# Attention scores from the fourth chunk on as float16 pairs over 64 rows, in a newly written order

## The chip, the cores and the metric

The kernel runs on one core of one Trainium2 chip. The metric is the device time of one execution in microseconds (us). The core has a matrix engine (TensorE, in the profile PE, its weight loads PEld), a vector engine (VectorE, DVE), a scalar engine (ScalarE, ACT), GpSimd (POOL) and a queue engine (SyncE, SP) which issues all transfers here.

## What is computed

The input is `q`, `k`, `v` of 4 batches, 8 heads, 768 positions, 64 channels. Each position attends to 96 local and 8 global positions; a two-layer network follows.

```
scores = q @ k.T / sqrt(64) + bias; scores = where(keep, scores, -1e9)
a = exp(scores - max); a = a / sum(a); attn = a @ v
x = attn as 3072 rows of 512
h = x @ w_in            # 512 x 2048
g = h * tanh(log(1 + exp(h)))
out = g @ w_out         # 2048 x 512
```

## The kernel before

The 3072 positions are 12 chunks of 256 (`ci`), three to a batch. A chunk has two halves of four heads, which are loaded apart (`G = 2*ci + g`: 24 loads of `q` and `k`), and eight score tiles `t`, so 96 in all: tile `t` belongs to chunk `t // 8`, and is for one pair of heads and one block of 128 queries. The pair's two heads lie on the two halves of the 128 partitions. For each head, `scores` multiplies 64 rows of `q` (128 columns, loaded as weights) with 64 rows of `k` (256 columns; 128 in the first block of a batch). One tile so takes two matmuls, one on each half of the rows, into two PSUM tiles `sc0` and `sc1`. Both are float32; each such matmul shows as two weight loads and two matmuls in the trace.

The other products take float16 pairs: a number is split into a high and a low float16 part, and high x high, high x low and low x high are added up in PSUM. Such is `weigh` (attention times `v`), `moe_in` (`ph`: 24 matmuls of 256 columns for a block `m`; 96 blocks, 8 to a chunk) and `moe_out` (`po`: 12 matmuls of 512 columns a block). The weights come as 64-bit numbers in 32 pieces of 512 KB and are turned to float16 pairs by `exponent_w`, `sign_w`, `join_w`, `high_w`, `low_w`, through four buffers each named `wc` and `ws`. Once the last piece is through, these buffers are idle.

No scheduler moves anything: every engine runs in the order of a written string, `PROGRAM`. A word is a letter and an index, a prime sends the step to DVE instead of ACT or POOL. The letters that matter here: `q` `v` `w` loads, `s` scores, `t` bias and row maximum (DVE), `y` exponential (ACT), `g` `p` high and low part of it, `X` its transposing transfer, `W` weigh, `A` to `E` the five steps of a weight piece, `i` moe_in, `o` moe_out, `z` `Z` high and low part of the activation, `L` `M` masks, `N` (new) their rescaling, `a` `b` (new) high and low part of `q`, `c` `d` (new) of `k`. The indices of `a` to `d` count from one more than `G`.

The first two chunks' blocks stand side by side: i0, i8, i1, i9 and so on to i7, i15; i16 and what follows is in rising order. By i16 all weight pieces are converted.

Of the kernel before, what the change touches and what calls it, by code (L numbers as in the profile page):

```python
# [114 lines left out]
def windowed(st, tc, loc):  # L115
# [88 lines left out]

    def split_v(ci):
        if ci < NC:
            for f in (high_v, low_v, window_v):
                f(ci)
# [36 lines left out]


# [256 lines left out]
    def flags():  # L503
# [25 lines left out]
        y15 W11 p13' g14 C4 X13 p14' D4 B5 A5 X14 t16 E4 i0 g15 q5 C5 y16 p15 D5 E5 W12 h2 X15 s17 j0 W13 l2 w6 W14 g16 R2 p16 x2 t17 T2 m0 s18 y17
        U2 X16 t18 u0 W15 R3 n0 s19 V2 y18 g17' T3' w7 r0 t19 p17 A6 w8 s20 U3 g18 X17 y19 G0 W16 t20 p18 V3 g19 H0 s21 y20 p19 X18 t21 z0 A7' s22  # L530
        y21 X19 B6 B7 w9 t22 Z0 W17 A8' g20 o0 C6 y22 w10 C7 D6' g21 D7' E6' w11 p21' i8 g22' B8 E7' A9 w12 B9 i1 C8 j8 C9 D8 w13 m8 A10 B10 u8 p20
        D9 s23 n8 p22' W18 w14 j1 W19 X20 t23 E9 r8 A11' y23 X21 m1 A12' G8 u1 X22 C10 n1 H8 E8 D10 r1 w15 i9 E10' A13 G1 z8 B11 A14 w16 g23 H1 Z8
        W20 j9 W21 p23' z1 i2 m9 X23 R4 Z1 u9 n9 B12 q6 T4 B13 W22 r9 U4 j2 G9 V4 m2 H9 u2 w17 W23 C11 z9 i10 B14 n2 Z9' A15 w18 C14 r2 D11 C13 D14
        s24 G2 j10 w19 R5 E11 D13 m10 o8 T5 E13' u10 H2 E14 w20 n10 t24 B15 r10 y24 o1 C12 w21 G10 z2 C15 A16 Z2' D12 A17 w22 H10 o9 A18 E12' D15
        z10' B16 g24 w23 B17 i3 B18 E15' w24 Z10' B19 i11 C18 j3 A19' w25 D18 m3 C16 u3 E18' D16 A20' n3 o2 p24' w26 C19 j11 X24 r3 U5 D19 m11 G3 V5
        u11 E19' o10 n11 H3 E16 r11 v3 C17 z3 B20 A21 i4 G11 A22 q7 A23 C20 D17 H11 Z3 D20 E17' z11 i12 q8 j4 E20' A24 B21 Z11' h3 C21 o3 m4 q9 D21
        A25' l3 u4 j12 E21' n4 x3 o11 m12 r4 B22 u12 B23 v4 n12 C22 r12 C23 s25 D22 G4 D23 E22' A26 H4 E23 t25 i5 z4 G12 y25 B24 g25 H12 Z4 w27 z12
        i13 C24 j5 Z12' D24 m5 B25 u5 B26 n5 w28 o4 C25 j13 w29 r5 C26 D25 B27 A27 G5 o12 w30 C27 D26' D27' m13 H5 E26 u13 z5 s26 E24' n13 A28' i6
        t26 Z5 r13 A29 G13 y26 B28 H13 E25 A30 w31 o5 j6 C28 g26 z13 m6 B29 D28 u6 Z13' i14 B30 n6 C29 r6 C30 D29' o13 D30' j14 G6 m14 H6 E30 u14 z6
        E28' s27 n14 Z6' i7 r14 q10 t27 p26 G14 y27 E27' g27' s28 j7 B31 o6 m7 p27' u7 H14 E29 n7 z14' r7 i15 A31' Z14' C31 G7 D31 h4' o14 H7 j15  # L540
        p25 l4 X25 z7 m15 X26 t28 E31 u15 i16 y28 Z7' X27 n15 r15 x4 g28' o7 p28 j16 G15 m16 H15 u16 v5 z15' n16 i17 Z15 Q0 r16 Y0 G16 s29 j17 H16
        o15 t29 z16' y29 m17 Z16' u17 g29 i18 n17 p29 Q1 r17 Y1 W24 G17 W25 j18 s30 X28 m18 W26 H17 u18 W27 X29 o16 t30 z17 n18 Z17 y30 r18 i19 g30
        G18 p30' H18 X30 z18' s31 j19 Z18 i20 t31 q11 m19 y31 u19 s32 g31 n19 W28 p31' W29 W30 j20 t32 o17 X31 r19 R6 y32 m20 T6 g32' G19 u20 s33 U6
        n20 o18 t33 V6 r20 H19 y33 G20 z19 p32' i21 Z19' X32 H20 g33' z20 p33' i22 Z20' j21 X33 m21 u21 n21 W31 r21 s34 R7 j22 o19 h5 t34 l5 y34 m22
        s35 x5 g34 T7' G21 u22 W32 o20 t35 p34 n22 H21 r22 q12 y35 U7 G22 z21 i23 g35' H22 p35 V7 z22 Z21' X34 Z22' s36 j23 o21 X35 m23 t36 u23 v6
        n23 y36 s37 r23 i24 t37 g36 p36 y37 G23 X36 g37 s38 H23 j24 p37 o22 t38 z23 Z23 y38 m24 g38' u24 i25 p38 n24 r24 G24 s39 H24 j25 o23 m25 q13
        z24 t39 u25 Z24 y39 n25 s40 g39' Q2 p39 i26 t40 r25 Y2 y40 G25 H25 s41 j26 z25' o24 m26 t41 Z25 u26 n26 y41 s42 r26 i27 t42 G26 y42 H26 z26
        i28 j27 Z26 m27 u27 s43 j28 W33 n27 m28 q14 W34 u28 W35 W36 r27 o25 n28 G27 X37 r28 H27 G28 X38 z27' i29 H28 Z27 X39 z28' Z28' i30 j29 g40
        m29 u29 p40 g41 n29 g42' W37 X40 t43 p41 W38 j30 o26 r29 R8 p42 y43 X41 G29 T8 X42 m30 U8 o27 u30 H29 V8 g43 n30 z29' p43 r30 Z29' s44 G30
        W39 W40 t44 X43 W41 i31 R9 y44 H30 g44' z30 T9' h6' s45 j31 Z30' W42 W43 l6 o28 t45 p44 x6 m31 y45 U9 X44 s46 u31 o29 g45 t46 V9 n31 p45'  # L550
        y46 v7 X45 r31 s47 g46 G31 o30 q15 t47 p46 H31 y47 z31' X46 Z31' i32 g47' p47' X47 s48 j32 i33 t48 m32 y48 u32 g48' p48' n32 s49 j33 o31 t49
        r32 m33 y49 G32 u33 H32 g49 W44 n33 p49 W45 X48 Q3 i34 R10 z32 X49 T10' r33 Z32 Y3 W46 G33 j34 W47 U10 o32 h7 m34 V10 H33 u34 l7 z33 n34 i35
        R11 Z33 x7 r34 G34 T11 H34 U11 v8 o33 z34 j35 V11 Z34 m35 u35 o34 n35 r35 G35 H35 i36 z35 Z35' i37 j36 m36 u36 n36 s50 r36 o35 j37 G36 m37
        H36 u37 t50 n37 z36' i38 r37 Z36' y50 G37 H37 g50' o36 z37' j38 p50 m38 X50 Z37' u38 i39 n38 r38 G38 H38 o37 j39 z38 m39 u39 Z38' n39 s51
        r39 i40 G39 q16 t51 H39 y51 i41 z39 g51' j40 p51 m40 X51 Z39 u40 o38 j41 n40 m41 u41 r40 n41 G40 W48 W49 W50 r41 H40 W51 s52 G41 i42 z40'
        t52 Z40 H41 y52 z41' g52' Z41' i43 j42 p52 m42 X52 u42 n42 o39 j43 r42 m43 u43 G42 n43 H42 s53 Q4 W52 z42' i44 t53 Z42 r43 Y4 y53 G43 H43
        g53 s54 p53 j44 o40 X53 m44 t54 u44 n44 y54 s55 z43 g54' o41 t55 q17 r44 p54 Z43' y55 G44 X54 g55 W53 H44 o42 p55' z44 R12 X55 Z44 T12 o43
        U12 V12 W54 i45 i46 j45 m45 u45 n45 W55 r45 s56 R13 h8 o44 G45 j46 T13 t56 H45 y56 s57 U13 z45 m46 i47 V13 t57 g56 u46 p56 y57 Z45' X56 n46
        s58 l8 g57 o45 r46 t58 p57 x8 j47 G46 y58 m47 H46 s59 u47 X57 g58 W56 z46' i48 t59 n47 Z46 q18 r47 p58 y59 G47 s60 X58 j48 g59' o46 H47 v9
        p59' z47 t60 X59 Z47' y60 i49 m48 u48 g60' p60' n48 X60 r48 W57 G48 j49 s61 m49 W58 H48 u49 o47 t61 n49 z48' r49 Z48 y61 i50 G49 Q5 g61' H49  # L560
# [200 lines left out]
```

## Time and profile before

| | |
|---|---|
| median of three runs | 677.55 us (677.5 to 678.16) |
| the profiled execution | 678.27 us |
| its span, first to last instruction | 676.4 us |
| PE busy | 627.8 us, 93% |
| DVE busy | 468.0 us, 69% |
| ACT busy | 450.0 us, 67% |
| POOL busy | 160.5 us, 24% |
| granted TensorE clock | full, but for part of 66.7 to 121.3 us and the last 8 us |

The difference of 1.9 us between execution and span lies before the first and behind the last instruction. A busy PE counts each matmul from start to modelled end, so that matmuls in a row overlap in that sum; their true spacing is read from the starts of groups in the timeline.

### The profile page before, as it was taken

What the parts mean: (1) busy time and instruction counts of PE and PEld (TensorE: products, weight loads), DVE (VectorE), ACT (ScalarE), POOL (GpSimd) and SP (SyncE); (2) the same over time, 40 slices, a digit from 0 to 9 for tenths busy, and PEclk for the clock granted to TensorE, in tenths of its full rate; (3) what the DMA queues carried; (4) which work ended last, traced back from release to release, by engine and by line L of the source; (5) the groups of instructions that cost most, each with busy time, mean ns of one, the idle gap of its engine ahead of it and who ended that gap; (6) DMA issues with size and microseconds to landing.
All of it is one profiled execution on the core that took longest, in us unless ns stands there. A gap on an engine that the chain in (4) does not pass through costs nothing.

```text
span 676.4 us, 13276 instructions
## 1 busy us (share of the span) xinstructions
PE 627.8 (93%) x4898; PEld 409.9 (61%) x4898; DVE 468.0 (69%) x1245; ACT 450.0 (67%) x1000; POOL 160.5 (24%) x140
## 2 busy tenths in 40 slices
...
GB/s 204 216 254 231 294 194 303 180 160 95 112 119 118 110 80 130 148 159 16 58 104 71 150 128 47 119 63 121 159 115 109 54 83 48 24 102 1 33 1 35
DMA packets 152680, 80.38 MB, mean 119 GB/s; under 512 B 121376, under 2 KB 141856, under 8 KB 152608
## 3 DMA queue, kind: packets, MB, share of 16 engines
...
q8 instruction: 40, 0.66, 0.4%
...
## 4 chain that ended last, share of the span: by engine, by line
PE 76%; DVE 13%; DMA 5%; SPq 3%; issue 2%; ACT 1%; POOL 0%; DVEq 0%; ACTq 0%; POOLq 0%
PE ph L438 32%; PE po L487 31%; PE sc L334 7%; DMA AT<-hl 4%; PE pav L393 4%; DVE r L465 2%; SPq L377 1%; DVE ws L294 1%; PE pav L487 1%; DVE A L348 1%; DVE gf L469 1%; DVE ws L288 1%; DVE ws L289 1%; DVE gt L153 1%; DVE wts L153 1%
## 5 line engine op out<-in xcount | busy, mean ns | idle before, releaser
L438 PE MATMUL ph<-xT,wts 128*128 128x256 f16 x2304 | 268.7, 275 | 11.2 <-DVE gmax L469 9.7
L438 PEld LDWEIGHTS <-wts 128*128 128x128 f16 x2304 | 224.9, 99 | 53.3 <-DVE gmax L469 8.3
L487 PE MATMUL po<-wts,gt 128*128 128x512 f16 x1056 | 242.5, 382 | 0.2 <-DVE wts L153 0.2
L487 PEld LDWEIGHTS <-gt 128*128 128x128 f16 x1152 | 109.2, 98 | 134.2 <-issue 14.2
L153 POOL TENSOR_TENSOR hl<-A,hl 128x512 f16<-128x512 f32 (+1 forms) x63 | 73.1, 1161 | 229.1 <-ACT hl L149 103.4
L465 DVE TENSOR_TENSOR r<-r,e 128x512 f32<-128x512 f32 x96 | 78.2, 815 | 57.7 <-ACT r L461 56.9
L153 POOL TENSOR_TENSOR gt<-gf,gt 128x512 f16<-128x512 f32 x56 | 68.0, 1213 | 208.2 <-ACT gt L149 95.0
L445 ACT ACTIVATE e<-ph 128x512 f32<-128x512 f32 x96 | 56.7, 591 | 82.2 <-PE ph L438 81.3
L357 ACT ACTIVATE A<-A,nm 128x256 f32<-128x256 f32 (+1 forms) x192 | 91.8, 479 | 26.1 <-DVE nm L348 24.8
L334 PE MATMUL sc<-kr,qr 64*128 64x256 f32 (+1 forms) x384 | 79.4, 468 | 17.5 <-DVE nm L348 10.1
L348 DVE CUSTOM_DVE_ANT_0 A<-sc,mb 128x256 f32<-128x256 f32 (+1 forms) x192 | 69.2, 396 | 26.8 <-PE sc L334 26.0
L449 DVE TENSOR_SCALAR e<-e 128x512 f32<-128x512 f32 x96 | 46.7, 487 | 55.9 <-ACT e L445 55.4
L453 ACT ACTIVATE u<-e 128x512 f32<-128x512 f32 x96 | 60.1, 626 | 36.2 <-DVE e L449 35.7
L457 ACT ACTIVATE r<-u,quarter 128x512 f32<-128x512 f32 x96 | 68.8, 717 | 2.1
L469 DVE CUSTOM_DVE_ANT_0 gf<-r,ph 128x512 f32<-128x512 f32 x96 | 65.5, 682 | 5.2 <-DVE r L465 1.9
L334 PEld LDWEIGHTS sc<-kr,qr 64*128 64x128 f32 x384 | 38.4, 212 | 42.8 <-DVE nm L348 16.4
L461 ACT ACTIVATE r<-r 128x512 f32<-128x512 f32 x96 | 60.0, 625 | 1.8
L393 PEld LDWEIGHTS <-AT 128*128 128x128 f16 x1056 | 39.7, 102 | 27.8 <-DMA AT<-hl 17.5
L149 ACT ACTIVATE gt<-gf 128x512 f16<-128x512 f32 x56 | 35.1, 626 | 18.6 <-DVE gmax L469 18.4
L393 PE MATMUL pav<-vc,AT 128*128 128x64 f16 x480 | 34.8, 200 | 9.8 <-DMA AT<-hl 9.4
L393 PE MATMUL pav<-vo,AT 128*128 128x64 f16 x576 | 39.9, 200 | 0.2 <-DMA AT<-hl 0.2
L357 ACT ACTIVATION_READ_ACCUMULATOR A<-A,nm 128x1 f32 x192 | 35.9, 187 | 0.0
...
## 6 DMA issues: line engine op xcount, KB each, us to landing
...
qr<-qT SPq DMA_DIRECT2D x24, 256.0 KB, 3.3
...
```

Source lines behind the costliest of these rows:

```text
L153: (nc.vector if other else nc.gpsimd).tensor_tensor(out, in_, high, op=ALU.subtract)
L334: nc.tensor.matmul(sc[j][:, 0:w], qr[half, a2, blk * P:(blk + 1) * P], kr[half, a2, col0:col0 + w], start=True, stop=True)
L348: nc.vector.tensor_tensor_reduce(out=A[:, j, 0:w], in0=sc[j][:, 0:w], in1=m, scale=-1.0 / UNIT, scalar=3.0e38, op0=ALU.add, op1=ALU.min, a ...
L357: nc.scalar.activation(A[:, j], A[:, j], AF.Exp, bias=nm[:, h:h + 1], scale=-1.0, accum_out=rs[:, h:h + 1])
L393: nc.tensor.matmul(pav[:, cols], AT[:, (x * 2 + j) * nk + kk, :], vs[kk][:, y, cols], start=(n == 0), stop=(n == last))
L438: nc.tensor.matmul(ph[:, j, :].rearrange("p (b t) -> p b t", b=2), wv4[:, 2 * fb, x, c * P:(c + 1) * P], xT[:, :, y * NCC + c, :], start=( ...
L453: nc.scalar.activation(u, mish[m]["e"], AF.Square)
L457: nc.scalar.activation(mish[m]["r"], mish[m]["u"], AF.Ln, bias=quarter, scale=1.0 / RS)
L461: nc.scalar.activation(r, r, AF.Exp, scale=-1.0)
L465: nc.vector.tensor_tensor(r, r, mish[m]["e"], op=ALU.mult)
L469: nc.vector.tensor_tensor_reduce(out=gf, in0=mish[m]["r"], in1=mish[m]["h"], scale=SG / (SV * SW * RS), scalar=0.0, op0=ALU.mult, op1=ALU. ...
L487: nc.tensor.matmul(pos[ci][t], gt[:, x, j, t * P:(t + 1) * P], wv4[:, 2 * fb + 1, y, :], start=(fb == 0 and n == 0), stop=(fb == NFB - 1 a ...
```

## The change

The first three chunks (24 tiles) keep float32 scores. From chunk 3 on (72 tiles), `q` is scaled by 256 and split into two float16 parts, `k` is split likewise, and each head's scores are three float16 matmuls over 64 rows, the two heads in turn. The parts lie in the buffers `ws` and `wc`. The bias masks are multiplied by 256 once, in place, when the 24th tile has been reduced. The two PSUM buffers of scores have one name instead of two. `PROGRAM` is written anew from its first word to its last.

```
+    CF32 = 3
+    WB = 4
+    def high_q(G, other=False):
+        both = mt.tile([P, DM], I32, name="ws", bufs=WB).bitcast(F16).rearrange("p (x a c) -> p x a c", x=2, c=CH)
+        split[G, "q"] = both[:, 0], both[:, 1]
+        copy(both[:, 0], raw[G][0], SQ, other)
+    def low_q(G):
+        qh, ql = split[G, "q"]
+        nc.vector.scalar_tensor_tensor(ql, raw[G][0], SQ, qh, op0=ALU.mult, op1=ALU.subtract)
+    def high_k(G, other=False):
+        o = first_key(G)
+        split[G, "k"] = tuple(mt.tile([P, DM], F32, name="wc", bufs=WB).bitcast(F16)[:, 0:GH // 2 * KW].rearrange("p (a w) -> p a w", w=KW) for x in range(2))
+        copy(split[G, "k"][0][:, :, o:], raw[G][1][:, :, o:], 1.0, other)
+    def low_k(G, other=False):
...
+        rest(kl[:, :, o:], raw[G][1][:, :, o:], kh[:, :, o:], other)
+    def units(i):
+        for m in (mb0, mb):
+            nc.vector.tensor_scalar(m, m, SQ, None, op0=ALU.mult)
...
-        sc = [ps.tile([P, W], F32, name=f"sc{j}", bufs=1) for j in range(2)]
-        for j in range(2):
-            half = slice(j * D, (j + 1) * D)
-            nc.tensor.matmul(sc[j][:, 0:w], qr[half, a2, blk * P:(blk + 1) * P], kr[half, a2, col0:col0 + w], start=True, stop=True)
+        if ci < CF32:
...
+            sc = [ps.tile([P, W], F32, name="sc") for j in range(2)]
+            for n, (x, y) in enumerate(((qh, kh), (ql, kh), (qh, kl))):
+                for j in range(2):
+                    half = slice(j * D, (j + 1) * D)
+                    nc.tensor.matmul(sc[j][:, 0:w], x[half, a2, blk * P:(blk + 1) * P], y[half, a2, col0:col0 + w], start=(n == 0), stop=(n == 2))
...
-        K0 v0 q0 K1 L5 q1 L7' L0' M3 L3' L4' M1 M2' M0' M6 L6' M4' M5 L1' L2' M7' h0 f0 q2 l0 s0 x0 t0 s1 y0 v1 t1 g0 s2 y1 p0' X0 t2 g1 p1 q3 s3 y2
+        K0 q0 q1 K1 L3 L4 L2 L1 L6' L5' M7' L7' L0' M0' M3' v0 M2' M1' M4' M6' M5' f0 q2 s0 t0 s1 y0 t1 g0 s2 y1 p0 q3 t2 g1 p1' s3 y2 h0' X0 t3 X1
```

What PE gets for one tile of scores of 256 columns, before (tile 34, with its neighbours `weigh` and `moe_out`; `kr`, `qr` are the float32 loads):

```order
L393 LDWEIGHTS AT_2435
L393 MATMUL pav1_2247<-vo_1556,AT_2435 128x64
L334 MATMUL sc0_2569<-kr_1543,qr_1542 128x256
L334 MATMUL sc1_2570<-kr_1543,qr_1542 128x256
L487 LDWEIGHTS gt_2483
L487 MATMUL po0_2278<-wts_102,gt_2483 128x512
```

And with the change, tile 26 with the rows next to it (`ws_1915` holds both parts of `q`, `wc_1902` the high and `wc_1903` the low part of `k`; `sc_2149` and `sc_2150` are the two heads' PSUM tiles):

```order
L369 LDWEIGHTS ws_1915
L369 MATMUL sc_2149<-wc_1902,ws_1915 128x256
L369 LDWEIGHTS ws_1915
L369 MATMUL sc_2150<-wc_1902,ws_1915 128x256
L369 LDWEIGHTS ws_1915
L369 MATMUL sc_2149<-wc_1902,ws_1915 128x256
L369 LDWEIGHTS ws_1915
L369 MATMUL sc_2150<-wc_1902,ws_1915 128x256
L369 LDWEIGHTS ws_1915
L369 MATMUL sc_2149<-wc_1903,ws_1915 128x256
L369 LDWEIGHTS ws_1915
L369 MATMUL sc_2150<-wc_1903,ws_1915 128x256
```

Two matmuls (four passes in the trace) became six, each with a weight load of its own, the two heads in turn.

On DVE, the place where the masks are rescaled, behind the reduction of tile 23 (`nm` and `A` are its; `ws` and `wts` a weight piece being joined and split; `hl` the parts of the exponentials, `e` block 8):

```order
L383 ISA A,nm_687<-sc,mb 128x256
L383 ISA nm_687 128x1
L321 SCALAR_TENSOR_TENSOR ws<-wc,ws 128x512 x2
L272 TENSOR_SCALAR mb_101<-mb_101 128x1024
L272 TENSOR_SCALAR mb<-mb 128x2048
L157 TENSOR_TENSOR wts<-ws,wts 128x512 x2
L157 TENSOR_TENSOR hl<-A,hl 128x512
L484 TENSOR_SCALAR e<-e 128x512
```

Two instructions of 1024 and 2048 columns are new there, ahead of the low parts of two weight pieces.

On ACT, the place of the first high part of `k` that waits for a buffer used before (`kr_1565` is the half G = 8; `r` and `e` are the network's, `A` exponentials, `gt` a high part):

```order
L392 ACTIVATE A_2174,rs1_2172<-A_2174,nm1_2173 128x256 x2
L488 ACTIVATE u_2183<-e_2170 128x512
L153 ACTIVATE gt_2195<-gf_2181 128x512
L492 ACTIVATE r_2223<-u_2183,quarter_88 128x512
L153 ACTIVATE wc_2228<-kr_1565 128x832
L496 ACTIVATE r_2223<-r_2223 128x512
L392 ACTIVATE A_2231,rs1_2172<-A_2231,nm1_2173 128x256 x2
```

The copy of 832 columns stands between two steps of one block of the network, and the next tile's exponentials stand behind it.

## Rows read from the trace of the kernel before

**Rows 1.** Windows, four stretches and the tail: stretch, its length, busy time of each engine.

```profile
0.00:77.40 77.40, 49.79 (x320) 30.70 (x321) 61.14 (x202) 49.45 (x136) 22.30 (x25) 0.91 1.04 227
77.40:174.10 96.70, 84.44 (x614) 55.29 (x613) 92.42 (x204) 69.47 (x132) 24.59 (x18) 0.95 0.69 197
174.10:224.60 50.50, 50.50 (x409) 32.81 (x407) 34.28 (x98) 38.37 (x90) 7.20 (x7) 1.00 0.52 123
224.60:668.40 443.80, 442.56 (x3558) 291.06 (x3556) 278.82 (x735) 292.04 (x641) 106.40 (x90) 1.00 0.37 83
668.40:676.40 8.00, 0.55 (x3) 0.09 (x2) 1.31 (x9) 0.69 (x2) 0.00 (x0) 0.80 0.21 75
```

**Rows 2.** Chain that ended last, 0 to 220 us: start, length, what.

```profile
19.44 5.19 DMA AT<-hl
...
182.05 0.42 PE sc L334 x4
...
189.58 2.59 PE po L487 x12
...
210.74 0.35 PE pav L393 x12
211.09 0.63 PE sc L334 x4
```

**Rows 3.** Chain that ended last, 640 us to the end.

```profile
652.97 2.62 PE ph L438 x24
655.59 12.96 PE po L487 x60
...
671.07 0.14 DVE done_i L78
```

**Rows 4.** Timeline of PE: first matmul of block 8, and block 16.

```profile
77.43 3.77 PE L438 MATMUL ph<-xT,wts 128*128 128x256 f16 x33
...
174.06 2.78 PE L438 MATMUL ph<-xT,wts 128*128 128x256 f16 x24
```

**Rows 5.** Timeline of PE, 220.7 to 231 us: score tiles of 256 columns.

```profile
220.65 0.70 PE L334 MATMUL sc<-kr,qr 64*128 64x256 f32 x4
221.28 2.76 PE L487 MATMUL po<-wts,gt 128*128 128x512 f16 x12
...
224.61 2.79 PE L438 MATMUL ph<-xT,wts 128*128 128x256 f16 x24
227.34 0.70 PE L334 MATMUL sc<-kr,qr 64*128 64x256 f32 x4
227.97 2.76 PE L487 MATMUL po<-wts,gt 128*128 128x512 f16 x12
```

**Rows 6.** Timeline of PE, 462 to 464 us: a score tile of 128 columns.

```profile
463.48 0.49 PE L334 MATMUL sc<-kr,qr 64*128 64x128 f32 x4
463.91 0.50 PE L438 MATMUL ph<-xT,wts 128*128 128x256 f16 x3
```

**Rows 7.** Groups by line and shape: busy, mean ns of one, idle before.

```profile
L438 PEld LDWEIGHTS <-wts 128*128 128x128 f16 x2304 | 224.9, 99 | 53.3 <-DVE gmax L469 8.3 <-issue 7.4 <-DVE wts L153 0.6
L334 PEld LDWEIGHTS sc<-kr,qr 64*128 64x128 f32 x384 | 38.4, 212 | 42.8 <-DVE nm L348 16.4 <-issue 10.1 <-DMA qr<-qT 7.4
L149 ACT ACTIVATE gt<-gf 128x512 f16<-128x512 f32 x56 | 35.1, 626 | 18.6 <-DVE gmax L469 18.4
L153 POOL TENSOR_TENSOR hl<-A,hl 128x512 f16<-128x512 f32 x52 | 64.6, 1243 | 187.2 <-ACT hl L149 76.3 <-DVE hl L147 51.5 <-issue 42.1
L294 DVE SCALAR_TENSOR_TENSOR ws<-wc,ws 128x512 int32<-128x512 int32 x32 | 21.5, 691 | 0.0
L153 DVE TENSOR_TENSOR wts<-ws,wts 128x512 f16<-128x512 f32 x18 | 13.4, 749 | 0.1
L288 DVE TENSOR_SCALAR ws<-wts 128x512 uint16<-128x512 uint16 x24 | 11.9, 497 | 0.0
L147 DVE TENSOR_SCALAR mb<-e 128x256 bf16<-128x256 f32 x4 | 1.1, 283 | 0.0
```

More of the change, by code (lines that the diff above doesn't have):

```diff
@@ L28 @@
 RS = 2.0 ** 8
+SQ = 256.0
 SV = 256.0
@@ L156, in windowed @@
     raw = {}
+    split = {}
     vraw = {}
@@ L165, in load_qk @@
         b, c = divmod(ci, NCHB)
+        o = OWN if c == 0 else 0
+        pairs = slice(g * GH // 2, (g + 1) * GH // 2)
         qr = raws.tile([P, GH // 2, CH], F32, name="qr", bufs=4)
         kr = raws.tile([P, GH // 2, KW], F32, name="kr", bufs=4)
-        o = OWN if c == 0 else 0
-        pairs = slice(g * GH // 2, (g + 1) * GH // 2)
         nc.sync.dma_start(qr, L.qT[b].rearrange("(a j) d s -> (j d) a s", j=2)[:, pairs, c * CH:(c + 1) * CH])
@@ L174, in load_qk, with first_key @@
         raw[G] = (qr, kr)
+    def first_key(G):
+        return OWN if (G // 2) % NCHB == 0 else 0
+    def high_q(G, other=False):
[10 more added lines that the diff above has]
+    def low_k(G, other=False):
+        o = first_key(G)
+        kh, kl = split[G, "k"]
+        rest(kl[:, :, o:], raw[G][1][:, :, o:], kh[:, :, o:], other)
     def load_v(ci):
@@ L203, in window_v @@
         vcmp[ci] = vc
[L205 to L208, printed above, removed]
     UNIT = L.ISC
@@ L272, in windowed @@
     wst = {}
-    WB = 4
     def exponent_w(i, other=False):
@@ L327, in scores @@
         ci, g, blk, a2, first, nk = shape(t)
-        qr, kr = raw[2 * ci + g]
         w = nk * P
         col0 = OWN if first else blk * STEP
-        sc = [ps.tile([P, W], F32, name=f"sc{j}", bufs=1) for j in range(2)]
-        for j in range(2):
-            half = slice(j * D, (j + 1) * D)
-            nc.tensor.matmul(sc[j][:, 0:w], qr[half, a2, blk * P:(blk + 1) * P], kr[half, a2, col0:col0 + w], start=True, stop=True)
+        if ci < CF32:
+            qr, kr = raw[2 * ci + g]
+            sc = [ps.tile([P, W], F32, name="sc") for j in range(2)]
+            for j in range(2):
+                half = slice(j * D, (j + 1) * D)
+                nc.tensor.matmul(sc[j][:, 0:w], qr[half, a2, blk * P:(blk + 1) * P], kr[half, a2, col0:col0 + w], start=True, stop=True)
+        else:
+            (qh, ql), (kh, kl) = split[2 * ci + g, "q"], split[2 * ci + g, "k"]
+            sc = [ps.tile([P, W], F32, name="sc") for j in range(2)]
+            for n, (x, y) in enumerate(((qh, kh), (ql, kh), (qh, kl))):
+                for j in range(2):
+                    half = slice(j * D, (j + 1) * D)
+                    nc.tensor.matmul(sc[j][:, 0:w], x[half, a2, blk * P:(blk + 1) * P], y[half, a2, col0:col0 + w], start=(n == 0), stop=(n == 2))
         pend[t] = sc
@@ L347, in largest @@
             m = mb0[:, h, :] if first else mb[:, h, :]
-            nc.vector.tensor_tensor_reduce(out=A[:, j, 0:w], in0=sc[j][:, 0:w], in1=m, scale=-1.0 / UNIT, scalar=3.0e38, op0=ALU.add, op1=ALU.min, accum_out=nm[:, h:h + 1])
+            nc.vector.tensor_tensor_reduce(out=A[:, j, 0:w], in0=sc[j][:, 0:w], in1=m, scale=-1.0 / (UNIT if ci < CF32 else UNIT * SQ), scalar=3.0e38, op0=ALU.add, op1=ALU.min, accum_out=nm[:, h:h + 1])
         pend[t] = A
@@ L515, in windowed @@
         "q": load_qk, "v": load_v, "w": load_w,
-        "h": high_v, "l": low_v, "x": window_v,
+        "a": lambda p, other=False: high_q(p - 1, other), "b": lambda p: low_q(p - 1), "c": lambda p, other=False: high_k(p - 1, other),
+        "d": lambda p, other=False: low_k(p - 1, other), "N": units, "h": high_v, "l": low_v, "x": window_v,
         "K": lambda i: masks_far() if i else masks_own(), "L": mask_own, "M": mask_far,
@@ L529, in windowed @@
[L529 to L560, printed above, removed]
@@ new lines, in windowed @@
+        y18 p16' D5 w7 T2' n0 t19 X16 r0 E5' W14 y19 U2 B6 V2 g17 A6' G0 s20 C6 w8 H0 p17 D6 z0 W15 E6' X17 g18 R3 Z0 t20 A7 o0 w9 T3' y20 B7 U3
+        g19' V3 p18' s21 C7 W16 X18 t21 p19 D7' s22 y21 w10 B8 X19 E7' W17 g20 t22 p20 s23 y22 A8' X20 B9 A9 t23 w11 C8 y23 i8 C9 D8 N0 D9 w12 g21
+        E8' A10 i1 E9' j8 p21' m8 g22 X21 B10 u8 p22' g23 W18 w13 C10 j1 W19 X22 W20 n8 p23' D10 m1 A11' r8 X23 B11 u1 G8 n1 C11 r1 H8 E10 w14 D11
+        i9 G1 z8 A12 E11' H1 w15 Z8' z1 W21 B12 A13 i2 j9 Z1' m9 R4 u9 w16 n9 B13 W22 T4 C12 W23 r9 U4 D12 w17 B14 A14 V4 R5 j2 C14 o8 T5 m2 A15 G9
@@ new lines, in windowed @@
+        D14 E12' w18 u2 E14' n2 H9 o1 r2 A16' B15 z9 w19 G2 C15 i10 H2 D15 Z9' z2 w20 E15' Z2' C13 o9 j10 B16 D13 w21 A17 m10 C16 u10 E13' D16 o2 U5
+        n10 E16' w22 A18 V5 B17 r10 A19 B18 i3 C17 C18 D17 G10 D18 w23 B19 E18' j3 C19 H10 E17 D19 w24 i11 z10 m3 B20 u3 Z10' n3 w25 B21 r3 o10 B22
+        j11 G3 m11 H3 E19 w26 u11 z3 i4 A20' B23 A21 A22 C20 A23 q6 C21 n11 C22 D21 Z3' r11 D22' o3 C23 j4 q7 A24 A25' m4 D23 G11 u4 E22 H11 D20
+        E23' n4 i12 q8 z11 E20' r4 Z11' A26 G4 B24 o11 j12 H4 E21 w27 z4 C24 m12 D24' u12 i5 Z4' n12 B25 q9 B26 r12 G12 o4 C26 j5 H12 E24 w28 z12
@@ new lines, in windowed @@
+        D26' m5 Z12' u5 i13 C25 A27 B27 n5 w29 E26 D25 r5 o12 C27 j13 G5 D27 w30 m13 H5 E25 u13 n13 i6 z5' E27' r13 v3 Z5' A28 G13 B28 o5 H13 j6 w31
+        C28 A29 m6 z13 B29 D28 Z13' u6 i14 C29 n6 B30 A30 D29' r6 C30 G6 o13 j14 D30' h3 m14 H6 E28 u14 E30' z6 n14 l3 i7 A31 r14 c7' x3 Z6' G14 v4
+        B31 a7 o6 j7 b7 m7 C31 u7 H14 d7 c8 n7 i15 z14' q10 r7 D31' Z14' G7 h4 d8' o14 j15 H7 E31 z7 m15 l4 u15 s24 n15 i16 Z7' x4 r15 t24 E29 y24
+        G15 a8 a9' v5 s25 a10 H15 o7 j16 b8 z15 g24' q11 t25 p24' y25 m16 b9 i17 u16 g25' X24 b10 Q0 p25' Z15' X25 n16 r16 s26 Y0 o15 j17 t26 G16
@@ new lines, in windowed @@
+        y26 m17 H16 u17 g26' s27 z16 i18 p26' n17 Z16' X26 c9 t27 r17 a11' y27 d9' s28 o16 j18 t28 q12 G17 y28 m18 H17 Q1 g27' s29 z17' i19 u18 t29
+        p27 Y1 g28 y29 Z17' X27 n18 b11 g29 p28 W24 r18 s30 p29' W25 X28 j19 o17 G18 t30 X29 H18 y30 m19 z18' u19 s31 Z18 i20 t31 a12 n19 c10' y31
+        b12 g30' r19 d10' W26 j20 W27 W28 g31' o18 q13 m20 G19 u20 p31 H19 n20 z19 p30 i21 r20 Z19' X30 G20 H20 X31 W29 s32 z20 R6 i22 j21 Z20 t32
+        T6 m21 y32 U6 W30 V6 u21 g32' s33 j22 o19 p32' n21 m22 X32 t33 u22 r21 y33 G21 W31 o20 H21 n22 g33' h5 R7 z21 l5 r22 i23 T7' x5 G22 U7 H22
@@ new lines, in windowed @@
+        Z21 W32 j23 s34 z22' V7 o21 p33' m23 Z22' u23 X33 t34 n23 v6 y34 s35 o22 t35 r23 g34' c11 G23 y35 a13' H23 p34 i24 g35 d11' X34 z23 Z23' q14
+        p35' o23 j24 b13 m24 u24 X35 n24 W33 Q2 i25 r24 Y2 G24 H24 W34 j25 s36 z24 i26 m25 t36 u25 Z24' n25 y36 W35 j26 s37 g36' r25 o24 m26 t37 p36
+        u26 n26 G25 X36 y37 H25 s38 r26 i27 g37' t38 z25 p37 G26 y38 X37 Z25 H26 g38 s39 j27 i28 p38' z26 m27 X38 c12 t39 Z26' u27 y39 d12 W36 s40
+        n27 o25 t40 g39 q15 r27 p39' y40 G27 H27 o26 j28 X39 g40 m28 z27' a14 p40 u28 b14 n28 X40 W37 Z27 W38 r28 R8 i29 G28 T8 H28 U8 z28 i30 j29
@@ new lines, in windowed @@
+        Z45' r46 a20 p63 W61 G46 j47 W62 X63 o45 m47 H46 u47 R14 n47 r47 z46' T14' s64 Z46' i48 t64 G47 y64 U14 H47 g64 V14 o46 j48 b20 z47 m48 p64
+        u48 n48 Z47 W63 X64 i49 r48 R15 G48 T15 h9' H48 o47 j49 l9 z48 m49 x9 U15 u49 Z48 W64 n49 V15 s65 Q5 i50 t65 v10 r49 Y5 y65 G49 H49 o48 j50
+        g65' z49 m50 p65 u50 n50 Z49' X65 s66 r50 i51 t66 G50 y66 H50 g66 z50' s67 j51 p66' o49 a21 m51 X66 t67 Z50 u51 n51 c19' b21 y67 W65 d19'
+        s68 r51 i52 t68 q22 g67 G51 y68 p67' H51 g68 X67 W66 j52 s69 p68 z51 i53 t69 Z51 X68 y69 m52 u52 g69' s70 p69 j53 o50 t70 n52 X69 m53 r52
@@ new lines, in windowed @@
+        u53 G52 y70 H52 s71 W67 n53 t71 i54 a22 z52' y71 b22 Z52 r53 g70 W68 g71' W69 j54 G53 s72 c20 m54 o51 H53 p70 u54 R16 z53 p71 X70 n54 t72
+        T16 Z53' i55 r54 X71 d20' y72 G54 q23 g72 U16 H54 p72 o52 j55 z54' X72 m55 Z54 u55 n55 V16 i56 r55 G55 H55 z55 W70 j56 i57 Z55 m56 u56 n56
+        W71 W72 j57 o53 R17 r56 m57 G56 u57 T17' n57 H56 o54 U17 r57 z56' V17 G57 h10' H57 Z56 i58 z57 l10 Z57 v11 i59 j58 x10 m58 u58 n58 s73 r58
+        o55 t73 j59 G58 y73 m59 H58 u59 g73' n59 i60 p73 Q6 z58' X73 Z58' r59 Y6 G59 s74 j60 o56 H59 m60 t74 u60 n60 y74 i61 z59' Z59' r60 g74 G60
```

63 lines of the change are left out of this document (35 added, 28 removed).

## The prediction, made before the changed kernel ran

> **What bounds the kernel now.** I first cut the execution where its character changes. The two cuts are the first matmuls of block 8 (77.4 us) and of block 16 (174.1 us) [rows 4]. The table by stretches [rows 1] then shows four stages. Up to 77.4 us transfers are the limit: the 16 transfer engines are booked at 1.04, DVE is busy for 61.1 us, and the chain of waits runs through transposing transfers of some 5 us [rows 2]. From there to block 16, DVE is busy for 92.4 of 96.7 us: it converts the weights, and PE waits for it. From 174.1 to 668.4 us PE is busy for 493.1 of 494.3 us, while DVE needs 313 and ACT 330. The last 8 us are the final copy, transfer and flags. So a microsecond less on PE is a microsecond less in the end only behind block 16, and one more on DVE costs only ahead of it.
>
> A busy PE may hide gaps, so I checked it against its spacing. The starts of groups that follow each other give 2.62 us for 24 matmuls of `ph`, 0.109 each; 12.96 for 60 of `po`, 0.216 each [rows 3]; 0.35 for 12 of `weigh`, 0.029 each [rows 2]. A tile of scores of 256 columns holds PE for 0.63 us [rows 2, 5]; the `ph` block ahead of it takes 2.73 instead of 2.62, so entering costs 0.10 more, and a tile costs 0.73. One of 128 columns takes 0.43 and 0.10, together 0.52 rounded down [rows 2, 6]. By these prices the work that the old program has from i16 on is 492.1 us. PE needed 494.3, so it really is the bound there, with about 2 us of waits.
>
> **What a tile costs with the change.** I split the 0.63 us. 128 columns less save 0.63 - 0.42 = 0.21 us over two passes [rows 2], so a pass streams 256 columns in 0.21, and something that does not depend on columns takes the other 0.105 of its 0.315. One after the other, the two heads' four passes would stream for 0.84 us, so the heads run at the same time on their halves of the rows. The fixed 0.105 I take for the float32 weight load, which lasts 212 ns where a float16 one lasts 99 [rows 7] and does not fit under the matmul ahead of it. Float16 loads do fit under one: `ph` has a load for each matmul of 256 columns and still goes at 0.109 each, and `weigh` at 0.029. So I price a pair of the new matmuls (both heads at once) at 0.109, leave 0.10 for entering and 0.105 once for leaving, and get 0.10 + 0.105 + 3 x 0.109 = 0.53, taken as 0.54 for the second head's offset. For 128 columns a pair is 0.058 (two loads at the 0.029 of `weigh`), which gives 0.38. A tile saves 0.19 or 0.14.
>
> No row shows a float16 matmul over 64 rows, so both ends matter. Cheapest, the fixed piece was all load, and nothing is paid once: 0.43, 0.10 less a tile. Dearest, each pair also waits for a float16 load of 0.098 that nothing hides: 0.10 + 3 x (0.107 + 0.098) = 0.72, and 0.56 for 128 columns, which saves nothing. I take 0.54, since the nearest float16 rows both hide their loads; the float32 rows are nearer only in the number of rows used.
>
> This is where the Trainium skill speaks against the change. "TensorE: Matmul & The Clock Gate", section "The mechanism", says that a weight load overlaps running matmuls only where it is for another group of rows. Each new pair's loads are for the row groups that are just in use, so by that sentence every pair pays its load, and the tile costs the 0.72 of the dearest end. The `ph` rows here disagree (every load is for all rows, and 0.109 leaves no room for one of 0.099); for 64 rows no run shows it.
>
> **Sum of the savings.** In the old program 29 tiles of scores stand ahead of i16, and 67 behind it (58 of 256 columns, 9 of 128). These save 58 x 0.19 + 9 x 0.14 = 12.3 us. The new program has 25 tiles ahead of i16. Four tiles (two of each size) thus leave a stage in which PE had time and enter one in which it has none: 2 x 0.54 + 2 x 0.38 = 1.8 us lost.
>
> **What the split costs.** Each of 18 halves of chunks has four new steps. High `q` is 512 columns: 0.63 us on ACT, 15 of 18 there. High `k` is 832 columns (576 in a batch's first chunk): the 0.63 scaled, some 1.0, 12 of 18 on ACT. Low `q`, always DVE: 0.69, as the join of a weight piece. Low `k`: POOL 1.24 x 832 / 512 = 2.0, nine times, or DVE 0.75 x 832 / 512 = 1.2, nine times [rows 7]. With the shifts of other steps between engines, issue times from i16 to the end grow by 33.7 us on DVE (356.6 to 390.3), by 20 on ACT and by 21 on POOL. Issue times overlap: 356.6 us made 314 of busy time in [rows 1], 0.88. So DVE rises to some 344 and ACT to some 350 of about 485 us, and PE covers them. The tightest stretch is i16 to i24: 56.9 us issued, about 49 busy on DVE, against 52 on PE. Without that cover DVE's 49 would push the end by little; a cumulative lag there is what I allow 1.5 us for. The new high `k` of a half must wait until the scores of two halves earlier have been read, since `wc` has four buffers and a half takes two. That wait stands on ACT, with a step of the network and the next exponentials behind it, and DVE and PE wait for those in turn. It costs nothing while the scores run ahead, as the order has them.
>
> **The start.** Up to i8 both programs issue nearly the same transfers (12 weight pieces, 6 loads of `q` and `k`, 3 of `v`; 21 transposes instead of 20), so the first stage cannot get much shorter than 77 us. DVE's issue time in it grows from 69.2 to 79.4: two more signs at 2 x 0.5, one join, two low parts of weights, more masks, a further reduction. At the same 0.88 that is 70 of 77 us busy, where 61 were. From i8 to i16 it falls from 110.3 to 107.8, the rescaling of the masks included. That is 3072 columns once, 3.4 us by the 283 ns for 256 [rows 7]; by 497 ns for 512 it would be 3.0. At 0.84, as measured there, this is 2 us less busy time. If DVE's waits in the first stage absorb all the extra work, block 16 starts at 172; if none, at 174.1 + 9 - 2 = 181. I take 175, since the extra work is there early and the stage has 16 us of waiting. PE and ACT have slack in both stages. The weights' last five loads now stand ahead of the transposes for chunk 3 on the transfer queue, which helps this stage and delays nothing that PE lacks before i16.
>
> **Sum.** Block 16 at 175; behind it 676.4 - 174.1 = 502.3, less 12.3, plus 1.8, plus 1.5 for waits: 668.3 us of span. Execution and span differ by 1.9, which gives 670.2, and the profiled execution lay 0.7 above the median: **669.5 us**.
>
> **Rivals.**
> 1. The loads are not hidden: 0.72 a tile. Savings are 58 x 0.01 - 9 x 0.04, about nothing, and the four moved tiles cost 2.6. The end is 175 + 502.3 + 2.6 + 1.5 + 1.2 = 682.6 us, slower. For it: the fixed 0.105 of every pass. Against it: `ph`, `po`, `weigh`. It decides from a tile of about 0.66 us, pairs of 0.15.
> 2. The start slips. DVE's waits are for data that come no earlier, block 16 starts at 181, and the time is 675.5. For it: DVE waits for transfers and scores at fixed places. Against it: 16 us to put 9 into.
> 3. ACT's new waits push exponentials behind PE. At 0.4 us for each of 18 halves the result is 676.7. Against it: ACT is free for a third of the time.
> 4. The heads share one rate. A float32 pass takes 0.21 us for 256 columns, twice what a float16 one does, so the rows don't show two heads at full rate. If pairs take 0.216, a tile costs 0.85, and the time is about 691.
> 5. The change does not do what it says: excluded, the order shows six float16 matmuls in each of 72 tiles.
>
> **How the numbers follow.** Forecast 0.64 (own range 661 to 675), rival 1 0.14, rival 2 0.12, rival 3 0.06, rival 4 0.04. The low end takes the cheapest tile (62 x 0.10 less) and block 16 at 172: 660. The high end includes rival 1. The range is 660 to 683, with rival 4 and half of the slips combined left out. About 0.2% can be told from no change in this kernel, so faster means below 676.2, slower above 678.9. Faster: the forecast, most of 2, half of 3, 0.74. Same: the rest of 2 and some of 3, 0.08. Slower: 1 and 4, 0.18.
>
> **What would show it.** In the timeline a tile of 256 columns spans about 0.43 to 0.45 us from its first matmul to the next group, six matmuls in pairs 0.109 apart; 0.6 speaks for rival 1, 0.75 for rival 4. Block 16 starts between 172 and 178. From there to the last matmul PE is busy for all but 4 us, DVE for about 344. More `sc` waits on PE for DVE or ACT behind block 16 would show rival 3. I am wrong if pairs are not hidden, or if the start takes longer than 180 us.

## The result, and the profile after

The changed kernel takes 670.48 us (670.1 to 670.73), the one before 677.84 in the same comparison: a ratio of 0.989 (0.987 to 0.991). The forecast was 669.5, within 660 to 683. The profiled execution took 670.73 us with a span of 669.0.

The table by stretches, cut as in [rows 1] at the first matmuls of block 8 (now at 80.2 us) and block 16 (now at 174.25), then at 226.75 and near the last matmul of `po`; the columns are stretch, length, busy time of PE, PEld, DVE, ACT and POOL, clock, share of the transfer engines and GB/s:

```profile
0.00:80.20 80.20, 51.51 (x325) 31.18 (x325) 66.20 (x213) 43.34 (x128) 20.33 (x23) 0.91 1.02 226
80.20:174.25 94.05, 80.81 (x596) 54.67 (x595) 91.20 (x189) 68.52 (x121) 22.57 (x12) 0.95 0.67 188
174.25:226.75 52.50, 52.37 (x455) 33.56 (x452) 47.02 (x129) 42.60 (x106) 10.46 (x8) 1.00 0.58 141
226.75:661.00 434.25, 431.11 (x3673) 285.14 (x3671) 310.07 (x762) 303.36 (x665) 128.09 (x101) 1.00 0.39 84
661.00:669.00 8.00, 0.41 (x2) 0.09 (x2) 1.30 (x9) 0.31 (x2) 0.00 (x0) 0.63 0.20 69
```

Block 16 starts where it did (174.25 after 174.06): the first stage is 2.8 us longer, the second 2.7 shorter. The whole gain lies behind it: 494.75 us instead of 502.3. PE is busy there almost throughout, as before. DVE is busy for 357 us, where it was 313. Up to the tail the granted clock by stretches is as before; in the old profile it was below full speed for parts of 62 to 110 us (the table of the profile before says 66.7 to 121.3).

The timeline of PE in the changed kernel (start, length, engine, line, operation, shapes, count), to set beside [rows 5, 6]:

```profile
179.85 2.78 PE L473 MATMUL ph<-xT,wts 128*128 128x256 f16 x24
182.56 0.50 PE L369 MATMUL sc<-wc,ws 64*128 64x256 f16 x6
183.00 2.76 PE L522 MATMUL pav<-wts,gt 128*128 128x512 f16 x12
185.69 0.50 PE L369 MATMUL sc<-wc,ws 64*128 64x256 f16 x6
186.13 2.79 PE L473 MATMUL ph<-xT,wts 128*128 128x256 f16 x24
188.85 0.34 PE L369 MATMUL sc<-wc,ws 64*128 64x128 f16 x6
189.13 2.76 PE L522 MATMUL po<-wts,gt 128*128 128x512 f16 x12
```

Read the starts. A tile of 256 columns runs from 182.56 to 183.00, 0.44 us where it was 0.63; one of 128 from 188.85 to 189.13, 0.28 where it was 0.43. In the medians of all float16 tiles behind block 16 the times are 0.434 and 0.274 us (0.635 and 0.424 before). The `ph` blocks ahead of them take 2.71 and 2.72 instead of 2.62, so entering still costs about 0.10. The tiles cost 0.53 and 0.37 in all, against 0.54 and 0.38 in the forecast.

The weight loads of the new tiles, in the groups by line and shape of the stretch from 174 to 661 us:

```profile
L369 PEld LDWEIGHTS <-ws 64*128 64x128 f16 x432 | 14.9, 94 | 18.1 <-issue 16.4
```

A load takes 94 ns. In the tile at 182.56 the second pair's loads start 11 and 15 ns behind the first pair's first matmul and run beside it, and the three pairs start at 0, 120 and 230 ns. So the loads are hidden, though they are for rows in use.

The new steps in the groups by line and shape (busy, mean ns of one, idle before):

```profile
L192 DVE SCALAR_TENSOR_TENSOR ws<-qr,ws 128x512 f16<-128x512 f32 x18 | 16.0, 888 | 1.3 <-ACT ws L153 1.3
L157 POOL TENSOR_TENSOR wc<-kr,wc 128x832 f16<-128x832 f32 x7 | 13.4, 1915 | 22.0 <-ACT wc L153 13.8 <-DVE wc L151 6.4 <-DMA AT<-hl 1.2
L157 DVE TENSOR_TENSOR wc<-kr,wc 128x832 f16<-128x832 f32 x5 | 5.1, 1016 | 0.0
L272 DVE TENSOR_SCALAR mb<-mb 128x2048 bf16<-128x2048 bf16 x1 | 0.7, 679 | 0.0
L272 DVE TENSOR_SCALAR mb<-mb 128x1024 bf16<-128x1024 bf16 x1 | 0.4, 414 | 0.0
```

### The profile page after: what moved, and what is told of

It is laid out like the page before. It is cut to its first block, busy times and chain, and to the rows that moved or that the text cites. A ratio compares the mean times of both kernels' runs of the same rounds, so it can differ in the third digit from the quotient of the medians.

```text
span 669.0 us, 13635 instructions
## 1 busy us (share of the span) xinstructions
PE 616.2 (92%) x5042; PEld 404.6 (60%) x5042; DVE 515.8 (77%) x1299; ACT 458.1 (68%) x1017; POOL 181.4 (27%) x143
## 5 line engine op out<-in xcount | busy, mean ns | idle before, releaser
L473 PE MATMUL ph<-xT,wts 128*128 128x256 f16 x2304 | 272.2, 276 | 14.7 <-DVE gmax L504 13.9
L157 POOL TENSOR_TENSOR hl<-A,hl 128x512 f16<-128x512 f32 (+1 forms) x64 | 77.5, 1215 | 204.5 <-DVE hl L151 60.0
L157 POOL TENSOR_TENSOR gt<-gf,gt 128x512 f16<-128x512 f32 x50 | 63.6, 1272 | 172.0 <-DVE gt L151 71.5
L484 DVE TENSOR_SCALAR e<-e 128x512 f32<-128x512 f32 x96 | 51.8, 540 | 23.8 <-ACT e L480 23.5
L362 PE MATMUL sc<-kr,qr 64*128 64x256 f32 (+1 forms) x96 | 31.4, 609 | 23.3 <-DVE nm L383 15.5
L157 POOL TENSOR_TENSOR wts<-ws,wts 128x512 f16<-128x512 f32 x13 | 23.4, 1808 | 67.1 <-ACT wts L153 43.5
L157 DVE TENSOR_TENSOR gt<-gf,gt 128x512 f16<-128x512 f32 x46 | 38.7, 842 | 1.6 <-ACT gt L153 1.4
```

What stands on the lines that cost most here:

```text
L157: (nc.vector if other else nc.gpsimd).tensor_tensor(out, in_, high, op=ALU.subtract)
L473: nc.tensor.matmul(ph[:, j, :].rearrange("p (b t) -> p b t", b=2), wv4[:, 2 * fb, x, c * P:(c + 1) * P], xT[:, :, y * NCC + c, :], start=( ...
L484: nc.vector.tensor_scalar(e, e, NTOP, 0.5, op0=ALU.min, op1=ALU.add)
```

## The experiments

Theory: the gain is the lower price of a tile on PE behind block 16, and the splits lie under PE. Rivals: the newly written order makes the gain, whatever the scores; or the splits take part of it back. Each ratio below is to runs of the kernel before on the same chip. A difference in us to the changed kernel is to its 670.48 us, which are of another comparison; the kernel before had between 676.98 and 677.84 us in them, so such a difference is good to about 1 us.

**The new order with the old scores.** Two kernels; the second also leaves out the split steps.

```
-    CF32 = 3
+    CF32 = 12
...
```

> As the kernel above, with the split steps taken out as well. Theory: the splits lie under PE, so this is 0 to 3 us less than the kernel above, 681 to 685. Rival (the splits load DVE and ACT so much that they eat part of the gain): 5 us or more less than the kernel above.

Measured without the splits: 679.06 us, ratio 1.002 (1.000 to 1.004). Block 16 starts at 170.7, and behind it PE is busy for 496.1 of 498.8 us, as its table by stretches shows:

```profile
0.00:170.70 170.70, 131.67 (x917) 85.68 (x917) 153.97 (x397) 112.49 (x248) 40.18 (x34) 0.94 0.83 206
170.70:669.50 498.80, 496.07 (x3984) 325.46 (x3982) 318.68 (x857) 334.17 (x743) 118.65 (x100) 1.00 0.39 90
```

So the new order alone gains nothing: with the old price of a tile, and loads moved to fit it, it is as slow as the old one. That rival falls. The 679 is a little below the expected 681 to 685, because the start, rid of the first splits and the mask step, was 3.5 us shorter than in the changed kernel.

> All 96 tiles have float32 scores, in the new order; the four split steps still run, but nobody reads their results; the masks are not rescaled, and a load of q and k comes later where its buffer is still in use. Theory (the tile's price on PE makes the gain): 60 tiles cost 0.20 us more and 12 cost 0.15 more, nearly all behind block 16: 670.5 + 13.8 = 684, 682 to 686. Rival (the new order makes the gain, whatever the scores): within 2 us of 670.5. Block 16 still starts at about 174 in both.

Measured with the splits kept: 702.3 us, ratio 1.037 (1.033 to 1.041). This one tells nothing on the price. Float32 scores hold the load buffers longer, so I had moved loads to later places, and ACT then waited 30 us for them, as the waits of ACT behind 174 us show (engine, line, waited for: us, times, longest):

```profile
ACT ws L153 <- DMA qr<-qT: 30.4, 11, 4.4
```

**What a pair costs.** The loop over the three products keeps only its first.

```
-            for n, (x, y) in enumerate(((qh, kh), (ql, kh), (qh, kl))):
+            for n, (x, y) in enumerate(((qh, kh),)):
...
```

> The changed kernel with only high x high in the scores of chunks 3 to 11: the two products with low parts are left out. Theory (PE is the bound, a pair costs 0.11): 60 x 0.22 + 12 x 0.12 = 14.6 us less, 656; up to 661 if DVE and ACT then hold PE up. Rival (a tile's price is mostly entering and leaving, or DVE is the bound): 665 or more.

Measured: 658.99 us, ratio 0.972 (0.970 to 0.975), 11.5 us below the changed kernel, in the theory's span. Its timeline has a tile of one pair followed by `po`:

```profile
549.88 0.28 PE L369 MATMUL sc<-wc,ws 64*128 64x256 f16 x2
550.09 2.76 PE L522 MATMUL po<-wts,gt 128*128 128x512 f16 x12
```

One pair holds PE for 0.21 us from its first matmul to the next group, three pairs for 0.44; by the medians (0.216 and 0.434) that is 0.109 a pair, and 0.107 that is paid once. PE is still close to being the bound with 14.6 us less to do, but 3 us of that do not arrive: in the profiled execution block 16 starts 1.5 us later, and PE stands for 5.0 us behind it where it stood for 2.9.

**Whether the heads overlap because they alternate.** The two loops are exchanged: three matmuls of one head, then three of the other.

```
-            for n, (x, y) in enumerate(((qh, kh), (ql, kh), (qh, kl))):
-                for j in range(2):
+            for j in range(2):
+                for n, (x, y) in enumerate(((qh, kh), (ql, kh), (qh, kl))):
```

> The changed kernel, but each tile issues the three matmuls of one head and then the three of the other. Theory (heads overlap because they alternate, matmuls start in program order): only the last of the first head and the first of the second overlap, five steps of 0.109 instead of three, 0.22 us more for 60 tiles and 0.11 for 12: 670.5 + 14.5 = 685. Rival 1 (the heads share the array anyway, no overlap at full rate): no change, 670.5. Rival 2 (PE reorders across rows): no change either, but pairs 4 ns apart in the trace.

Measured: 670.05 us, ratio 0.989 (0.986 to 0.992): no change, so my expectation was wrong. Its timeline of PE:

```profile
399.76 0.83 PE L369 MATMUL sc<-wc,ws 64*128 64x256 f16 x6 [0.26 <-DVE nm L383]
400.52 2.79 PE L473 MATMUL ph<-xT,wts 128*128 128x256 f16 x24
...
407.01 0.51 PE L369 MATMUL sc<-wc,ws 64*128 64x256 f16 x6
407.45 2.76 PE L522 MATMUL po<-wts,gt 128*128 128x512 f16 x12
```

The tile at 407.01 takes 0.44 us, as with the heads alternating, though the program has them one after the other. With 0.107 for leaving, six matmuls of 0.109 in a row would be 0.76, and five steps 0.65. The six start at 0, 10, 120, 130, 230 and 240 ns, so the fourth in the program starts second. In one of the 72 tiles, at 399.76, the second head's buffer came late: there the six start in the program's order and take 0.76. (The same tile takes 0.76 in the changed kernel too.) So matmuls of the second head run beside those of the first where their buffers are free, ahead of earlier ones of the first head. This is rival 2 of the expectation, with pairs 10 ns apart and not 4. Rival 1 (one shared rate) would give 0.76 for three pairs and falls.

**Two tiles in one visit.** Both tiles of a block issue their twelve matmuls together, into one PSUM tile for each row half.

```
...
+        elif a2 == 0:
+            sc = [ps.tile([P, 2, W], F32, name="sc") for j in range(2)]
+            for a in range(2):
...
+                        nc.tensor.matmul(sc[j][:, a, 0:w], x[half, a, blk * P:(blk + 1) * P], y[half, a, col0:col0 + w], start=(n == 0), stop=(n == 2))
...
```

> The changed kernel, where the float16 scores of two tiles (both pairs of heads of a block) are issued together into one PSUM tile for each row half, at the place of the first. Theory (entering and leaving the 64-row form costs 0.10 each, once a visit): 36 x 0.19 = 6.9 us less, 663.6, up to 666 with new waits. Rival (the 0.20 belongs to the tile, not to the visit, or the score buffers then hold PE up): 670 or more.

Measured: 664.34 us, ratio 0.982 (0.979 to 0.984), 6.1 us below the changed kernel. In its timeline twelve matmuls take 0.77 us, from 440.78 to 441.55, where two tiles apart take 2 x 0.44 and enter twice:

```profile
440.78 0.83 PE L371 MATMUL sc<-wc,ws 64*128 64x256 f16 x12
441.55 2.76 PE L524 MATMUL po<-wts,gt 128*128 128x512 f16 x12
```

The price of 0.10 on each side belongs to the visit. This version beats both kernels.

**The old order with the new scores.** The string of before, with the split steps put between (high parts behind the second tile of the half before, low parts behind the third), float16 from chunk 4 on.

```
-    CF32 = 3
+    CF32 = 4
...
-        K0 q0 q1 K1 L3 L4 L2 L1 L6' L5' M7' L7' L0' M0' M3' v0 M2' M1' M4' M6' M5' f0 q2 s0 t0 s1 y0 t1 g0 s2 y1 p0 q3 t2 g1 p1' s3 y2 h0' X0 t3 X1
+        K0 v0 q0 K1 L5 q1 L7' L0' M3 L3' L4' M1 M2' M0' M6 L6' M4' M5 L1' L2' M7' h0 f0 q2 l0 s0 x0 t0 s1 y0 v1 t1 g0 s2 y1 p0' X0 t2 g1 p1 q3 s3 y2
...
```

> The order of before, word for word, with the split steps and the rescaling put in between: float16 scores from chunk 4 on (64 tiles), float32 in chunk 3, so that nothing is split while weights are converted. Theory (price of a tile alone): 56 x 0.20 + 8 x 0.15 = 12.4 us less than before, 665.4, and 1 to 3 us of new waits: 666 to 669. Rival (the gain needs the new order): 672 or more.

Measured: 677.98 us, ratio 1.002 (1.001 to 1.004). The theory failed here. Two tiles in one visit change nothing on top of it:

> The old order with float16 from chunk 4, and two tiles issued together as in the kernel above. Theory: 32 x 0.19 = 6.1 us less than the old order with float16, 660 to 663. Rival: no gain over it.

Measured: 678.38 us, ratio 1.002 (1.001 to 1.003). PE was no longer the bound in this order: with one tile a visit it stands for 10.7 us behind block 16. So I took the splits away: the later chunks read chunk 4's parts, and the output is then not the function's.

```
-            (qh, ql), (kh, kl) = split[2 * ci + g, "q"], split[2 * ci + g, "k"]
+            (qh, ql), (kh, kl) = split[8 + g, "q"], split[8 + g, "k"]
...
```

> The old order with float16 scores from chunk 4, where only chunk 4 is split and all later chunks' scores read its parts: the splits of chunks 5 to 11 are left out. If the splits, put where I put them, held PE up in the old order with float16 scores: 666 to 669. If the order itself does, whose steps on DVE and ACT stand so that a tile has the old 0.73 us: 674 to 678.

Measured: 665.84 us, ratio 0.984 (0.982 to 0.986), which is the 665.4 of the price alone. Behind block 16 PE stands for 2.1 us. The stretch from 230 to 450 us in the table by stretches, first with the splits, then (second fence) without them:

```profile
230.00:450.00 220.00, 214.49 (x1879) 142.06 (x1877) 153.22 (x383) 155.68 (x346) 65.98 (x53) 1.00 0.45 99
```

```profile
230.00:450.00 220.00, 219.18 (x1933) 145.78 (x1931) 146.56 (x385) 151.13 (x338) 55.03 (x48) 1.00 0.44 98
```

With the splits DVE is busy for only 70% of the stretch, and PE still stands for 5.5 us. So DVE's sum of work does not explain it. What I conclude, without having tried other places, is that the place of the splits in the two in-order engines does. The waits of PE's loads behind 174 us say for what, again with the splits first and then without:

```profile
PEld L473 <- DVE gmax L504: 11.5, 15, 2.2
```

```profile
PEld L473 <- DVE gmax L504: 2.3, 3, 1.6
```

`ph` has two PSUM buffers, and a block can start when DVE has read the one before the last (`gmax` is written by that step). A split ahead of that step on DVE, or ahead of an ACT step that it needs, can so come out on PE. The trace bears this out in part: 8 of the 15 waits, 7.1 of the 11.5 us, have a split on DVE or ACT in the 6 us before them. Why the others are late stays open. ACT's waits in this run have none for a buffer of the splits.

**What the splits cost in the new order.** Left out from chunk 5 on (as above, with chunk 4's parts read instead), and, in another kernel, each split step run twice.

> The changed kernel, where the splits of chunks 5 to 11 are left out and their scores read chunk 4's parts. If the waits for DVE behind block 16 (some 4 us more than before) come from the splits: 666 to 668. If from the order: 670.

Measured: 667.57 us (665.73 to 668.59), ratio 0.985 (0.984 to 0.987), 2.9 us below the changed kernel (2.5 by the ratios). The waits of PE's loads for `ph` behind 174 us, in the changed kernel and then in this one:

```profile
PEld L473 <- DVE gmax L504: 4.9, 10, 0.9
```

```profile
PEld L473 <- DVE gmax L504: 2.5, 4, 1.3
```

> The changed kernel with every split step run twice in a row, the same values again: some 25 us more issue time on DVE, 17 on ACT, 17 on POOL. Theory (the splits lie under PE behind block 16): 670.5 to 674. Rival (DVE and ACT are so near to the bound that the splits hold PE up): 677 or more.

```
...
-        a8 a9' v5 s25 a10 H15 o7 j16 b8 z15
+        a8 a8 a9' a9' v5 s25 a10 a10 H15 o7 j16 b8 b8 z15
...
```

Measured: 703.14 us, ratio 1.038 (1.037 to 1.040): 33 us more, at the rival's end. In its profile block 16 starts 4.2 us later; behind it PE stands for 24.0 us where it stood for 2.9, and is busy for 7.8 us longer with the same matmuls. Three stretches of the changed kernel and then the same of this one:

```profile
174.00:230.00 56.00, 55.87 (x484) 36.34 (x484) 50.52 (x136) 44.62 (x109) 10.69 (x8) 1.00 0.57 138
230.00:450.00 220.00, 217.39 (x1965) 144.71 (x1964) 180.41 (x442) 167.64 (x386) 69.30 (x53) 1.00 0.56 119
450.00:655.00 205.00, 204.89 (x1659) 135.43 (x1657) 126.41 (x316) 132.88 (x274) 58.43 (x47) 1.00 0.22 49
```

```profile
174.00:230.00 56.00, 51.36 (x427) 33.06 (x426) 51.97 (x127) 41.03 (x99) 10.43 (x8) 0.97 0.50 115
230.00:450.00 220.00, 205.25 (x1820) 133.76 (x1819) 187.05 (x438) 166.59 (x379) 73.28 (x54) 0.98 0.54 113
450.00:655.00 205.00, 200.34 (x1660) 132.57 (x1658) 137.44 (x331) 136.18 (x285) 62.09 (x49) 1.00 0.26 60
```

The changed kernel has DVE busy for 82% of the middle stretch and PE waits little. At 85% PE stands for 15 us. At 215.5, 273.5 and 338.4 us, each time after PE had stood for some us, the granted clock falls from full speed (2.4 GHz) to half (1.2 GHz) for a while, which gives the 0.97 and 0.98 of the first two stretches. The splits lie under PE only just.

**The waits for buffers, and DVE's share.**

```
+    WC = 5
...
-        c = mt.tile([P, DM], F32, name="wc", bufs=WB)
+        c = mt.tile([P, DM], F32, name="wc", bufs=WC)
```

> The changed kernel with five wc buffers instead of four. Theory (the high parts' waits for buffers cost nothing): 670.5 within 0.6. Rival (these waits on ACT are the 3 us of waits by which the steady part exceeds the sum): 668 or less.

Measured: 669.9 us (667.94 to 671.87), ratio 0.990 (0.988 to 0.992): no change that can be told, as expected. The splits' waits for buffers on ACT were short in the changed kernel:

```profile
ACT ws L153 <- PE sc L369: 1.0, 2, 0.8
ACT wc L153 <- PE sc L369: 0.4, 1, 0.4
```

The last kernel issues two tiles together and has all low parts of `k` on POOL.

> The changed kernel with two tiles issued together, and all 18 low parts of k on POOL instead of nine on DVE: some 10 us less on DVE, 17 more on POOL. If DVE's lag makes the rest of PE's waits: 661 to 663, against 664.3 with nine on DVE. If POOL's longer steps delay the low parts of the activation behind them: 665 or more.

```
...
-        G7 h4 d8' o14 j15
+        G7 h4 d8 o14 j15
...
```

Measured: 665.95 us, ratio 0.982 (0.980 to 0.984), the same as with nine on DVE within the intervals (0.979 to 0.984). Moving low parts to POOL gains nothing. It does not free DVE either: behind block 16 DVE is busy for 353.7 us, with nine of them on DVE for 355.5. The timeline of the changed kernel shows what may be the reason (POOL and DVE):

```profile
272.57 1.52 POOL L157 TENSOR_TENSOR wc<-kr,wc 128x576 f16<-128x576 f32 x1 [1.19 <-ACT wc L153]
272.88 1.77 DVE L192 SCALAR_TENSOR_TENSOR ws<-qr,ws 128x512 f16<-128x512 f32 x1
```

This low part of `q` takes 1.77 us, in the median it takes 0.68. Behind block 16 of the changed kernel 58 of 320 steps of DVE (the network's scaling and products, and the high and low parts) take over 1.3 times the median of their kind, and every one of the 58 overlaps a step of POOL. Together they run 42 us over their medians. Before, these were 31 steps and 20 us, with POOL busy for 114 us instead of 139. No run tests whether POOL is the cause.

## Why the prediction was right, point by point

**The bound, and the price of a tile.** Both held. PE bounds everything behind block 16, before and after, and a tile's price fell from 0.73 to 0.53 us (0.54 predicted) and from 0.52 to 0.37 (0.38). The pair's 0.109 is shown by the kernel with one product, entering and leaving by the one with two tiles in a visit. The 0.105 for leaving had no row of its own in the prediction; 0.107 is what one pair's 0.216 leaves. Float16 loads of 94 ns over 64 rows hide under matmuls of the same rows, in pairs 0.109 apart. That settles rival 1, and with it the sentence of the Trainium skill that I weighed ("TensorE: Matmul & The Clock Gate", "The mechanism"): here the measurement decides against that sentence. Rival 4 is settled by the same 0.109: both heads run at full rate.

**The start.** Block 16 was put at 175 and came at 174.25, though not quite as I had it. In the first stage DVE was busy for 5.1 us more (66.2; I had put 70), but only 2.3 of that went into its waits, and the stage became 2.8 us longer. The second stage gave these back: it became 2.7 us shorter, 1.2 of them less work of DVE and 1.4 less waiting. That the two cancel so closely is luck. The rescaling of the masks was priced at 3.4 us from float32 rows; in bfloat16 it took 1.1. Rival 2 did not come about.

**Behind block 16.** I had 12.3 us of savings, less 1.8 for four moved tiles, less 1.5 for waits: 9.0. Measured are 7.5. By the prices now measured, the savings are 58 x 0.20 + 9 x 0.15 = 13.0 and the moved tiles cost 1.8, so PE's work from block 16 is 480.9 us. It took 486.3 to the end of the last `po` (at 660.6), which makes some 5 us of waits where the old program had 2; the tail behind it became 0.5 us longer. The term that was too small is the 1.5 us for waits: it measured 3. The kernel without the later splits, 2.9 us faster, shows that these waits come from the splits.

**The cover.** The step that reads best and held worst is "PE covers them". I reasoned from DVE's total (344 of 485 us predicted, 357 of 487 measured; the steps stretched beside POOL are enough for the 13 us). I also wrote that a microsecond more on DVE costs only ahead of block 16, and that does not hold: behind it the later splits cost 2.9 us, and all splits run twice add 29 there. The old order with the splits has DVE less busy than the changed kernel and loses all 12 us. Rival 3 had the mechanism, a split ahead of a step that PE waits for, though mainly through DVE's reading of `ph` and not through buffer waits on ACT (1.4 us in all, and a fifth buffer changes nothing), and its price depends on the order: 0.2 us for each half of chunks 5 to 11 in the new one, 0.9 in the old one as I placed them. So the rewritten order makes no gain of its own, but in the old order, with the splits in the one placement that I tried, the cheaper tile gains nothing. Whether a good placement in the old order would keep the 12 us was not tried.

**What stays open.** How far the float32 kernel with the splits kept (702.3 us) was held up by the moved loads and how far by the splits was not separated. Nor was how much of DVE's longer time comes from POOL's added steps.
